# Row halves that exchange gate and up: a fused attention and feed-forward kernel

## The chip, the cores and the metric

The kernel runs on one core of a Trainium2 chip. Five engines work side by side from their own instruction queues: TensorE (PE in the profile; its weight loads are listed as PEld), VectorE (DVE), ScalarE (ACT), GpSimd (POOL) and SyncE (SP, which here only issues DMAs). They wait for each other through semaphores. The metric is the device time of one execution in microseconds. In the profile a line such as L375 is line 375 of the kernel before.

## The reference

```python
x = A_x                                   # [1, 2048, 448], bf16
xn = _layernorm(x)                        # (x - mean) / sqrt(var + 1e-5), no weights
# A: 16 query heads, 8 key/value heads, head size 256, the last W = 512 cached keys
q = (xn @ wq)                             # wq [448, 4096]
p = softmax(q k^T / 16)                   # over 512 keys, no mask
s = (p v) @ wo                            # wo [4096, 448]
# B: feed-forward, width 1792
g = silu((gelu_tanh(xn @ w_gate) * (xn @ w_up)) @ w_down)
return x + s * g
```

The inner size 448 is 3 x 128 + 64, or 7 x 64. That remainder is what the change is about: the array of TensorE has 128 rows.

## The kernel before, in words

The 2048 rows of x are cut into NQC = 4 chunks of QC = 512 rows, each of TPC = 4 tiles of 128. The program is recorded as a list of operations by `Rec.op`, one queue per engine, in the order in which the code issues them. `Rec` works out the semaphore waits from the tiles that an operation reads and writes; an operation on PE never waits for an earlier one on PE. Nothing reorders the work later, so the order in the code is the order on each engine.

*Start.* Four DMAs bring the tiles of chunk 0. DVE takes the statistics of all four (L293, L294), ACT the roots in two pairs (L335), and DVE the reciprocals (L338) and the normalized tiles (L299). PE, which has run 12 matmuls on zeros (`warm`, L308), transposes each tile with 14 transposes of 64 columns (L321), so that `xnT` holds each piece of 64 rows twice: on partitions 0 to 63 and again on 64 to 127. ACT copies two tiles out of PSUM (L327) and DVE two (L329). SP meanwhile issues the loads of the gate and up weights in four slices (`load_gu`, L238), gate to partitions 0 to 63 and up to 64 to 127, then w_down and the later chunks of x.

*Feed-forward, per chunk.* `gate_up(c, f)` handles one of NF = 14 blocks of 128 columns. For each of NK = 7 pieces of 64 rows it issues two matmuls (L375): gate in the lower row half of the array into one PSUM bank, up in the upper half into the next bank. The two run side by side. Three pairs of banks are used in turn. ACT applies gelu (L379) and DVE multiplies (L381). `down(c, t)` (L387) then makes the output of four tiles in banks 6 and 7. The later chunks are normalized on DVE among these blocks (`ln_later`, `ln_later2`), with GpSimd for the inverse root; DVE writes two copies of each normalized tile, and a transposing DMA issued by SP (L241) fills `xnT` in both halves. GpSimd issues the loads of wq, v and wo (`load_piece`) at fixed places, kept in step by a wait for PE.

*Attention.* Each of 64 (chunk, head) pairs has four slots, one for a tile of 128 queries: `scores` (L433, banks 4 and 5 in turn), the exponential with its sum on ACT (L437), reciprocal and scaling on DVE (L439, L440), a transposing DMA by SP, and, some 12 slots later, `values` (L453, mostly banks 0, 1 and 6) with a copy on DVE (L459), then `outproj` (L473, bank 7). `q_burst` projects queries in bursts of 4 or 8 half-pairs of heads, again with 7 pairs of 64-row matmuls (L418), two heads in the two row halves, into banks 0 to 3; ACT copies two banks at once (L422). The `down` tiles of the last chunk are put among slots 0 to 11 and 16 to 23 of this stage, in banks 6, 7, 7 and 2.

Of the kernel before, what the change touches and what calls it, by code (L numbers as in the profile page):

```python
# [11 lines left out]
P = 128  # L12
# [10 lines left out]
class Rec:  # L23
# [41 lines left out]
    def op(self, eng, fn, r=(), w=(), dma=False, after=(), lane=None):  # L65
# [17 lines left out]
        for d, raw in deps:  # L83
            if d.eng == eng and not d.dma and not dma and (eng == "tensor" or not raw and eng != "gpsimd"):
                continue
            d.inc = d.waited = True
            o.deps.append(d)
# [54 lines left out]
def bass_recurrent_scan__sliding_block_cached__geglu_ffn__prompt_kernel(nc, A_x, A_k, A_v, A_wq, A_wo, B_x, B_wg, B_wu, B_wd, out):  # L142
# [6 lines left out]
    QC, TPC, HP = 512, 4, 64  # L149
    NQC = S // QC  # L150
    NT = NQC * TPC
    NK = D // HP
    NF, NJ, NE = F // P, W // P, Dh // P
    assert S % QC == 0 and D % HP == 0 and NE == 2 and NJ == 4 and Hq == 2 * Hkv and Hq % 4 == 0 and NF % 2 == 0
# [4 lines left out]
    with es:  # L159
# [20 lines left out]
        xnT, _ = sb("xnT", [P, NQC, NK, QC], BF16)  # L180
# [3 lines left out]
        wq, _ = sb("wq", [P, NK, Hkv, Dh], BF16)  # L184
        wo, _ = sb("wo", [P, Hq * NE, D], BF16)
        gu_at = off[0]
        wgu, x_at = sb("wgu", [P, NK, F], BF16)
        x4, _ = sb("x4", [P, NT, D], BF16)
        NX = 4
        xn2, d_at = sb("xn2", [P, NX, NK, 2, HP], BF16)  # L190
# [16 lines left out]
        def fill_pr(at, end):  # L207
            while at + 2 * W <= end:
                t_, at = sb("pr%d" % len(pr), [P, W], BF16, at)
                pr.append(t_)  # L210
# [7 lines left out]
        for n in range(3, NQP):  # L218
            qT[n], at = sb("qT%d" % n, [P, 2, NE, QC], BF16, at)
        assert at >= hb_at, (at, hb_at)  # L220
        fill_pr(at, nc.sbuf_usable_end)
# [22 lines left out]
        dve(lambda e: e.memset(actT[:, NF - 1, :], 0.0), w=[("actT", NF - 1)])  # L244
# [8 lines left out]
        x0 = [dma("sync", x4[:, t, :], x_view[:, 0, t, :], w=[("x4", t)]) for t in range(TPC)]  # L253
        wg_v = B_wg.rearrange("(k p) f -> p k f", p=HP)
        wu_v = B_wu.rearrange("(k p) f -> p k f", p=HP)
        cuts = [0, 2, 6, 10, NF]
        fslice = {f: s for s in range(4) for f in range(cuts[s], cuts[s + 1])}

        def load_gu(s):
            a, b = cuts[s] * P, cuts[s + 1] * P  # L260
            dma("sync", wgu[0:HP, :, a:b], wg_v[:, :, a:b], w=[("wgu", 0, s)])
            dma("sync", wgu[HP:P, :, a:b], wu_v[:, :, a:b], w=[("wgu", 1, s)])
# [6 lines left out]
        for sl in range(4):  # L269
            load_gu(sl)  # L270
            if sl == 1:
                load_x(1)
        dma("sync", wd[:, :, :], B_wd.rearrange("(f p) d -> p f d", p=P), w=[("wd",)])
        for c in range(2, NQC):
# [5 lines left out]
        wq_v = A_wq.rearrange("(k p) (g two m) -> p k g two m", p=HP, two=2, m=Dh)  # L280
        pieces = [(wq[lo * HP:(lo + 1) * HP, k, :, :], wq_v[:, k, :, lo, :], ("wq", lo, k))
                  for k in range(NK) for lo in range(2)]
# [13 lines left out]
        def ln_norm(t, copies=2):  # L296
            s = t % NX
            for o in range(copies):
                dve(lambda e, o=o: e.tensor_scalar(  # L299
                    xn2[:, s, :, o, :], x4[:, t, :].rearrange("p (k d) -> p k d", k=NK), mv[:, t, 0:1],  # L300
                    rstd[:, t:t + 1], op0=ALU.subtract, op1=ALU.mult),
                    r=[("x4", t), ("mv", t), ("rstd", t)], w=[("xn2", s, o)])

        def warm(n):

            def run(e):
                for _ in range(n):
                    ins = e.matmul(bank(3), lhsT=actT[:, NF - 1, 0:P], rhs=actT[:, NF - 1, :], start=True, stop=True)  # L308
# [3 lines left out]
        def ln_tr(t):  # L312
            parts = ((act, 4),), ((dve, 5),), ((act, 6),), ((dve, 7),)
            parts = [(eng, b, 0, NK) for eng, b in parts[t]]
            for eng, b, a, z in parts:
                tp = bank(b).bitcast(BF16)

                def tr(e, tp=tp, a=a, z=z):
                    for k in range(a, z):
                        for lo in (0, HP):  # L320
                            ins = e.transpose(tp[lo:lo + HP, (k - a) * P:(k - a + 1) * P], xn2[:, t, k, 0, :], ident[:, :])  # L321
                    return ins
                pe(tr, r=[("xn2", t, 0), ("ident",)], w=[("ps", b)])
                dst = xnT[:, 0, a:z, t * P:(t + 1) * P]
                src = tp[:, 0:(z - a) * P].rearrange("p (k q) -> p k q", q=P)
                if eng is act:
                    act(lambda e, dst=dst, src=src: e.activation(dst, src, ACT.Copy), r=[("ps", b)], w=[("xnT", 0, t, a)])  # L327
                else:
                    dve(lambda e, dst=dst, src=src: e.tensor_copy(dst, src), r=[("ps", b)], w=[("xnT", 0, t, a)])  # L329

        for t in range(TPC):
            ln_stats(t)
            if t % 2:
                a, b = t - 1, t + 1
                act(lambda e, a=a, b=b: e.activation(std[:, a:b], mv[:, a:b, 1], ACT.Sqrt, bias=small[:, 0:1]),  # L335
                    r=[("mv", a), ("mv", t), ("eps",)], w=[("std", a)])
        for a in range(0, TPC, 2):
            dve(lambda e, a=a: e.reciprocal(rstd[:, a:a + 2], std[:, a:a + 2]),  # L338
                r=[("std", a)], w=[("rstd", a), ("rstd", a + 1)])
            ln_norm(a, 1)  # L340
# [262 lines left out]
```

## Time and profile before

| what | us |
|---|---|
| median of 3 runs (lowest to highest) | 559.74 (559.12 to 559.98) |
| the profiled execution: its own time | 558.75 |
| its span, first to last instruction | 557.0 |
| PE busy | 548.7 |
| DVE / ACT / POOL busy | 324.1 / 296.3 / 89.7 |
| gate/up of one chunk on the chain (196 matmuls) | 21.26 |
| down of one chunk (56 matmuls) | 10.70 |
| a burst of 8 on the chain (112 matmuls) | 12.19 |
| start of the first gate/up matmul | 9.28 |

Busy time counts an engine's instructions; matmuls are pipelined, so PE's share says that it never lacks work, not that it runs at its peak. The chain that ended last is followed back from the last instruction to what released each step. Lines of it are "start, length, what". Idle time of engines other than PE costs nothing as long as PE has its operands.

### The profile page before, as it was taken

Reading aid. Unit: us, or ns where it says so; the run is one execution under the profiler, and the core shown is the slowest. Engines: PE = TensorE matmul, PEld = TensorE weight load, DVE = VectorE, ACT = ScalarE, POOL = GpSimd, SP = SyncE. Lnnn points to the kernel's source line nnn. Section 1 sums busy time; section 2 is a strip of 40 time slices with the busy share of each in tenths; the row PEclk is TensorE's granted clock in tenths of the full one; section 3 lists DMA queues with packets and bytes.
Section 4 is the critical chain, followed back from the end, with each engine's and each line's share of the span. In section 5 each row is a group of like instructions: output and inputs, shape, how many; then the busy total and the mean of one; then the engine's idle time right before and its main releaser. Section 6 shows DMA issues by size and latency. Waiting matters only on the chain.

```text
span 557.0 us, 9857 instructions
## 1 busy us (share of the span) xinstructions
PE 548.7 (99%) x3498; PEld 258.8 (46%) x3532; DVE 324.1 (58%) x835; ACT 296.3 (53%) x673; POOL 89.7 (16%) x125
## 2 busy tenths in 40 slices
PE   8999999999999999999999999999999999999997
PEld 4544444444444444444444444444444444444445
DVE  5727446143462688078728744782688078638774
ACT  4423233247746665655575656556665655565631
POOL 0232323200000121001411110042121002411123
PEclk9999999999999999999999999999999999999999
DMA  8996846932453365245535542445354254634552
GB/s 196 276 177 102 138 102 143 264 110 70 95 87 67 67 96 98 46 94 104 112 81 95 104 86 44 100 92 137 75 96 100 34 95 97 120 88 98 93 95 52
DMA packets 169552, 58.83 MB, mean 106 GB/s; under 512 B 160160, under 2 KB 166432, under 8 KB 169504
## 3 DMA queue, kind: packets, MB, share of 16 engines
q1 hardware_dynamic: 166208, 45.50, 44.3%
q0 software_dynamic: 3152, 12.65, 8.7%
q8 instruction: 28, 0.46, 0.4%
q14 instruction: 20, 0.16, 0.1%
q10 hardware_dynamic: 144, 0.06, 0.0%
HBM read 17.92 MB, written 1.84 MB: 35 GB/s over the span
## 4 chain that ended last, share of the span: by engine, by line
PE 97%; DVE 2%; issue 1%; DMA 0%; ACT 0%
PE ps L453 20%; PE ps L433 20%; PE ps L418 18%; PE ps L473 17%; PE ps L375 15%; PE ps L387 8%; DVE tmp L482 0%; DVE xr L484 0%; DVE stats L293 0%; DMA x<-in_A_x_dram 0%; PE ps L321 0%; ACT xnT L327 0%; DVE mv L294 0%; DVE xn L299 0%; DVE rstd L338 0%
## 5 line engine op out<-in xcount | busy, mean ns | idle before, releaser
L437 ACT ACTIVATE pr<-ps 128x512 bf16<-128x512 f32 x256 | 152.7, 597 | 121.4 <-PE ps L433 117.9
L433 PE MATMUL ps<-kT,qT 128*128 128x512 bf16 x493 | 147.7, 379 | 2.0 <-issue 1.4
L453 PE MATMUL ps<-pT,V 128*128 128x512 bf16 x497 | 129.1, 379 | 0.8
L439 DVE RECIPROCAL rden<-den 128x1 f32<-128x1 f32 x256 | 41.5, 162 | 148.2 <-ACT pr L437 129.8
L473 PE MATMUL ps<-wo,oT 128*128 128x448 bf16 (+1 forms) x536 | 116.2, 344 | 0.0
L440 DVE TENSOR_SCALAR pr<-pr,rden 128x512 bf16<-128x512 bf16 x256 | 108.0, 422 | 9.0
L418 PE MATMUL ps<-xnT,wq 64*128 64x512 bf16 x896 | 98.3, 376 | 0.0
L422 ACT ACTIVATE qT<-ps 128x1024 bf16<-128x1024 f32 x64 | 65.5, 1023 | 40.6 <-PE ps L418 40.6
L375 PE MATMUL ps<-xnT,wgu 64*128 64x512 bf16 x784 | 85.3, 376 | 0.8 <-ACT xnT L327 0.8
L459 DVE CAST oT<-ps 128x512 bf16<-128x512 f32 x124 | 84.5, 682 | 0.7 <-PE ps L453 0.5
L453 PEld LDWEIGHTS ps<-pT,V 128*128 128x128 bf16 x512 | 50.0, 98 | 60.2 <-issue 0.3
L473 PEld LDWEIGHTS ps<-wo,oT 128*128 128x128 bf16 x536 | 52.4, 98 | 51.0
L433 PEld LDWEIGHTS ps<-kT,qT 128*128 128x128 bf16 x512 | 49.1, 98 | 55.8 <-issue 4.5
L381 DVE TENSOR_TENSOR actT<-ps,hb 128x512 bf16<-128x512 f32 x56 | 38.1, 685 | 57.2 <-ACT hb L379 55.3
L418 PEld LDWEIGHTS ps<-xnT,wq 64*128 64x128 bf16 x896 | 43.0, 94 | 54.6 <-DVE acc L494 2.5
L379 ACT ACTIVATE hb<-ps 128x512 bf16<-128x512 f32 x56 | 33.4, 597 | 51.4 <-PE ps L375 51.4
L375 PEld LDWEIGHTS ps<-xnT,wgu 64*128 64x128 bf16 x784 | 39.4, 94 | 46.0 <-issue 1.6
L437 ACT ACTIVATION_READ_ACCUMULATOR pr<-ps 128x1 f32 x256 | 49.8, 195 | 0.0
L387 PE MATMUL ps<-wd,actT 128*128 128x448 bf16 x224 | 46.2, 353 | 0.1
L498 POOL TENSOR_TENSOR tmp<-acc,gy 128x448 f32<-128x448 f32 x16 | 16.5, 1034 | 158.6 <-DVE acc L494 158.6
L513 POOL TENSOR_SCALAR tmp<-tmp 128x448 f32<-128x448 f32 x16 | 9.0, 563 | 187.8 <-ACT tmp L512 187.8
L387 PEld LDWEIGHTS ps<-wd,actT 128*128 128x128 bf16 x224 | 21.7, 98 | 22.2 <-issue 1.3
(43 smaller groups left out, 172.4 us busy)
## 6 DMA issues: line engine op xcount, KB each, us to landing
pT<-pr SPq DMA_TRANSPOSE x256, 2.4
wq<-in_A_wq_dram POOLq DMA_DIRECT2D x14, 256.0 KB, 5.2
wo<-in_A_wo_dram POOLq DMA_DIRECT2D x4, 896.0 KB, 6.6
V<-in_A_v_cache_dram POOLq DMA_DIRECT2D x4, 512.0 KB, 5.0
xr<-in_A_x_dram POOLq DMA_DIRECT2D x4, 448.0 KB, 3.9
wd<-in_B_w_down_dram SPq DMA_DIRECT2D x1, 1568.0 KB, 18.5
wgu<-in_B_w_gate_dram SPq DMA_DIRECT2D x3, 448.0 KB, 9.5
wgu<-in_B_w_up_dram SPq DMA_DIRECT2D x3, 448.0 KB, 11.1
```

The source lines that it names most:

```text
L375: ins = e.matmul(bank(b), lhsT=wgu[lo:lo + HP, k, f * P:(f + 1) * P], rhs=xnT[lo:lo + HP, c, k, :], start=k == 0, stop=k == NK - 1)
L381: dve(lambda e: e.tensor_tensor(actT[:, f, :], bank(s + 1), hb[:, n % NHB, :], ALU.mult), r=[("ps", s + 1), ("hb", n % NHB)], w=[("actT", f)])
L387: pe(lambda e, f=f: e.matmul(bank(b, D), lhsT=actT[:, f, t * P:(t + 1) * P], rhs=wd[:, f, :], start=f == 0, stop=f == NF - 1), r=[("actT", ...
L418: ins = e.matmul(bank(b), lhsT=wq[lo:lo + HP, k, h0 // 2 + hp, e_ * P:(e_ + 1) * P], rhs=xnT[lo:lo + HP, c, k, :], start=k == 0, stop=k == ...
L422: act(lambda e, e_=e_, s=s, buf=buf: e.activation(buf[:, :, e_, :], psum[:, s * 512:(s + 2) * 512].rearrange("p (a q) -> p a q", a=2), ACT ...
L433: ins = e.matmul(bank(b), lhsT=buf[:, a, k, t * P:(t + 1) * P], rhs=kT[:, g, k, :], start=k == 0, stop=k == NE - 1)
L437: act(lambda e: e.activation(pr[s][:, :], bank(b), ACT.Exp, scale=scale, accum_out=den[:, s:s + 1]), r=[("ps", b)], w=[("pr%d" % s,), ("de ...
L439: dve(lambda e: e.reciprocal(rden[:, s:s + 1], den[:, s:s + 1]), r=[("den", s)], w=[("rden", s)])
L440: dve(lambda e: e.tensor_scalar(pr[s][:, :], pr[s][:, :], rden[:, s:s + 1], None, op0=ALU.mult), r=[("pr%d" % s,), ("rden", s)], w=[("pr%d ...
L453: ins = e.matmul(bank(b), lhsT=V[:, j, g, e_ * P:(e_ + 1) * P], rhs=pT[:, i % NPT, j, :], start=j == 0, stop=j == NJ - 1)
L459: dve(lambda e: e.tensor_copy(dst, bank(b)), r=[("ps", b)], w=[key])
L473: ins = e.matmul(bank(b, D)[:, lo:hi], lhsT=oT[G % 2][:, idx, t * P:(t + 1) * P], rhs=wo[:, h0 * NE + idx, lo:hi], start=idx == 0, stop=id ...
```

## The change

The number of matmuls of each kind stays as it is, apart from the transposes and the warm-up. What changes:

- *Layout.* The first 384 of the 448 rows of gate, up and wq lie as three pieces of 128 rows on all partitions; the last 64 rows of gate (or of the first head) lie on partitions 0 to 63 and of up (or of the second head) on 64 to 127. `xnT` has four pieces instead of seven; only the last 64 rows are held twice.
- *Two phases.* A block runs phase 0: for each of the four pieces, gate on the lower row half and up on the upper half. Phase 1 covers the three full pieces with the halves exchanged, and adds into the same two banks. Phase 1 of a block is issued after phase 0 of the next, and waits for the end of its own phase 0 (`hard`). Four pairs of banks are used in the feed-forward, three in bursts of 8.
- *Start.* x comes in three DMAs. The first two tiles are normalized on GpSimd as soon as their own statistics are ready, the others on DVE. Transposes are 5 a tile, in banks 6 and 7 alone; ACT copies tiles 0 and 1, DVE 2 and 3. The warm-up is 50 matmuls of 128 columns. The weights come in three slices, with the last 64 rows in loads of their own.
- *Later chunks.* DVE writes one normalized copy; ACT copies its last 64 columns; `ln_later` and `ln_later2` move to other blocks.
- *Last chunk's down tiles.* Banks 6, 7, 3, 7; the last two tiles move from slots 16 to 23 to slots 13 to 20.
- *Memory.* Twelve buffers for probabilities; qT3 lies behind the feed-forward buffers.

```diff
-    def op(self, eng, fn, r=(), w=(), dma=False, after=(), lane=None):
+    def op(self, eng, fn, r=(), w=(), dma=False, after=(), lane=None, hard=()):
...
+        for d in hard:
+            d.inc = d.waited = True
+            o.deps.append(d)
...
-        xnT, _ = sb("xnT", [P, NQC, NK, QC], BF16)
+        xnT, _ = sb("xnT", [P, NQC, KF + 1, QC], BF16)
-        wq, _ = sb("wq", [P, NK, Hkv, Dh], BF16)
+        wq, _ = sb("wq", [P, KF, Hq, Dh], BF16)
+        wq6, _ = sb("wq6", [P, Hq // 2, Dh], BF16)
-        wgu, x_at = sb("wgu", [P, NK, F], BF16)
+        wg, _ = sb("wg", [P, KF, F], BF16)
+        wu, _ = sb("wu", [P, KF, F], BF16)
+        wgu6, x_at = sb("wgu6", [P, F], BF16)
-        xn2, d_at = sb("xn2", [P, NX, NK, 2, HP], BF16)
+        xn2, d_at = sb("xn2", [P, NX, D + HP], BF16)
...
-        dve(lambda e: e.memset(actT[:, NF - 1, :], 0.0), w=[("actT", NF - 1)])
+        dve(lambda e: e.memset(actT[:, NF - 1, 0:P], 0.0), w=[("actT", NF - 1)])
...
-        for sl in range(4):
-            load_gu(sl)
-            if sl == 1:
-                load_x(1)
+        load_x0(0, 1)
+        load_x0(1, 2)
+        load_x0(2, TPC)
+        load_gu6(0, 3)
+        load_gu(0)
+        load_gu6(3, NF)
+        load_gu(1)
+        load_x(1)
+        load_gu(2)
...
+        def ln_norm(t, eng=dve):
+            eng(lambda e: e.tensor_scalar(xn2[:, t % NX, 0:D], x4[:, t, :], mv[:, t, 0:1], rstd[:, t:t + 1],
+                                          op0=ALU.subtract, op1=ALU.mult),
+                r=[("x4", t), ("mv", t), ("rstd", t)], w=[("xn2", t % NX, 0)])
...
+        def ln_tr(t):
+            b = 6 + t % 2
+            tp = bank(b).bitcast(BF16)
+            def tr(e):
+                for k in range(KF):
+                    e.transpose(tp[:, k * P:(k + 1) * P], xn2[:, t, k * P:(k + 1) * P], ident[:, :])
+                for lo in (0, HP):
+                    ins = e.transpose(tp[lo:lo + HP, KF * P:(KF + 1) * P], xn2[:, t, KF * P:D], ident[:, :])
+                return ins
+            pe(tr, r=[("xn2", t, 0), ("ident",)], w=[("ps", b)])
...
+        def ln_first(t):
+            dve(lambda e: e.reciprocal(rstd[:, t:t + 1], std[:, t:t + 1]), r=[("std", t)], w=[("rstd", t)])
+            ln_norm(t, pool if t < 2 else dve)
+        warm(44)
+        ln_stats(0)
+        ln_std(0)
+        for t in range(1, TPC):
+            ln_stats(t)
+            ln_std(t)
+            if t < 3:
+                ln_first(t - 1)
+        for t in range(2, TPC):
+            ln_first(t)
+        warm(6)
+        ln_tr(0)
+        ln_copy(0)
...
+        def two_blocks(ph, c, s, w, w6, keys, q0=0, q1=QC):
+            def run(e):
+                for k in range(KF + 1 - ph):
+                    for lo in (0, HP):
+                        m = (lo > 0) ^ ph
+                        lhsT = w[m][lo:lo + HP, k, :] if k < KF else w6[lo:lo + HP, :]
+                        ins = e.matmul(bank(s + m)[:, q0:q1], lhsT=lhsT, rhs=xnT[lo:lo + HP, c, k, q0:q1],
+                                       start=ph == 0 and k == 0, stop=ph == 1 and k == KF - 1)
+                return ins
+            hard = [phase0[s]] if ph else []
+            phase0[s] = pe(run, r=xn(c)[q0 // P:q1 // P] + keys, w=[("ps", s), ("ps", s + 1)], hard=hard)
...
-            b = (6, 7, 7, 2)[t] if c == NQC - 1 else 6 + t % 2
+            b = (6, 7, 3, 7)[t] if c == NQC - 1 else 6 + t % 2
...
+            for n in range(heads + 1):
+                if n < heads:
+                    part(n, 0)
+                if n:
+                    part(n - 1, 1)
...
-            lead = 4 if c == 0 else 1
-            for f in range(NF):
-                gate_up(c, f)
...
+            lead = 6 if c == 0 else 2
+            for f in range(NF + 1):
+                if f < NF:
+                    gate_up(c, f, 0)
+                if f:
+                    gate_up(c, f - 1, 1)
...
-        for d, slots in ((0, range(0, 4)), (1, range(4, 12)), (2, range(16, 20)), (3, range(20, 24))):
+        for d, slots in ((0, range(0, 4)), (1, range(4, 12)), (2, range(13, 17)), (3, range(17, 21))):
```

## The prediction

> **What bounds the kernel now.** First the busy shares and the chain that ended last, to see which engine sets the time.
>
> ```profile
> span 557.0 us, 9857 instructions
> ...
> PE 548.7 (99%) x3498; PEld 258.8 (46%) x3532; DVE 324.1 (58%) x835; ACT 296.3 (53%) x673; POOL 89.7 (16%) x125
> ...
> PE 97%; DVE 2%; issue 1%; DMA 0%; ACT 0%
> ```
>
> PE is the whole chain. A change can help only by shortening PE's stream, by closing holes in it, or by starting it earlier. Next the chain in order of time over the first stage, which shows what PE waits for before its stream begins.
>
> ```profile
> 0.73 2.06 DMA x<-in_A_x_dram
> ...
> 5.92 0.52 DVE xn L299
> 6.44 0.04 issue
> 6.48 0.99 PE ps L321 x28
> 7.48 0.03 issue
> 7.51 0.60 PE ps L321 x14
> 8.11 0.02 issue
> 8.13 0.93 ACT xnT L327
> 9.06 0.22 issue
> 9.28 6.85 PE ps L375 x61
> ```
>
> The same chain over the whole span then shows stages without holes:
>
> ```profile
> 9.28 21.33 PE ps L375 x196
> 30.60 10.70 PE ps L387 x56
> 41.30 21.26 PE ps L375 x196
> ...
> 170.02 12.19 PE ps L418 x112
> ```
>
> The stream of useful matmuls starts at 9.28 us. From there 196 gate/up matmuls take 21.26 us: 98 pairs, one in each row half, at 0.217 us a pair. The projections of q run at 12.19 us for 112, 0.218 a pair. So both are bound by the columns streamed. The last view is the list of waits:
>
> ```profile
> PEld ps L433 <- ACT pr L437: 1.0, 4, 0.4
> ...
> PEld ps L375 <- ACT xnT L327: 0.9, 1, 0.9
> ```
>
> (total, times, longest). PE's weight loads for the scores wait for exponentials four times, all between 130 and 154 us and partly beside matmuls still streaming. Later only short holes at the changes between 64-row and 128-row operands remain, and those stay in number.
>
> **The pieces.** A block of 128 columns of gate and up had 7 pairs (NK = 7); now it has 4 in phase 0 and 3 in phase 1, again 7 with 512 columns each. So 392 pairs of L375 and 448 of L418 stay, and steady PE time moves by 0. That is the largest fact about this change.
>
> **The new wait.** Phase 1 of a block waits for its own phase 0 on PE's semaphore (120 waits: 56 blocks of the FFN, 64 of q). Behind it on PE are its 12 weight loads and matmuls and everything later; gelu (L379) or the copy of q (L422) waits for them. Between stands the next block's phase 0 and the previous block's phase 1, 7 pairs or 1.52 us; at the ends of a run 4 pairs (0.87) or 3 (0.65). A matmul of that kind ends 0.376 us after its start, 0.16 after its columns are in. So the wait is over 0.5 us before its turn in the tightest place. Before, the same engine waits for the product of the block three earlier (DVE L381), which ends 0.6 + 0.69 + about 0.15 us after the block's own pairs, about 1.6 us before the third next block begins, and the 21.26 us show no hole. I take 0; the upper end is a full exposed hand-over per wait, about 0.1 us (the chain has 0.06 of issue at 152.85, after a release that came just in time), 12 us in all; below 0 nothing, since a wait gains nothing.
>
> **The start.** I rebuild the chain. The first tile of x arrives at 2.79 as before. DVE's statistics come every 0.72 us (0.52 + 0.18 + 0.02 in the chain): mean and variance of tile 0 at 3.66, tile 1 at 4.38. Tile 0's root (ACT, 0.30) is under tile 1's statistics, its reciprocal ends near 4.45, and GpSimd normalizes it from 4.5. The cost there is not in the trace: nearest is GpSimd's tensor_scalar on 128x448 (L513, 563 ns), the other end its tensor_tensor (L498, 1034 ns). I take 0.56 (same kind): tile 0 ready at 5.1, tile 1 at 5.9; with 1.03 they are ready at 5.5 and 6.6. Queued behind it on GpSimd is nothing before the statistics of chunk 1. DVE meanwhile does the statistics of tiles 2 and 3 (to about 6.05, with two reciprocals) and norms 2 and 3 (0.5 each): 6.65 and 7.2, where the last norm before ended at 7.87.
>
> PE's warm-up goes from 12 matmuls of 512 columns to 50 of 128, all ahead of the transposes. The 512-column ones come every 0.43 us until the array's clock rises, so 0.107 each; the twelve took 4.95 us, less than 12 x 0.427 = 5.12, so the rise is near 5.7. From 1.05 (the memset is halved) 43 slow ones reach 5.65 and seven at half the time end near 6.05. All slow: 6.4. With a rise at 4.5: 5.5. So the first transpose goes at 6.05 and not at 5.1, and the early GpSimd norms are mostly wasted; 0.43 us ahead of today's 6.48 remain.
>
> A tile now has 5 transposes instead of 14; the row is 0.63 us from the first (6.48) to the copy that it releases (7.11). I take 0.5, ends 0.25 and 0.63. ACT's copy drops from 896 to 512 columns: 0.917 to about 0.60 (L379 reads 128x512 in 597 ns). DVE's drops from 620 ns to 0.42 (in proportion 0.35, unchanged 0.62). But only banks 6 and 7 are used: transposes of tile 2 wait for ACT's copy of tile 0, those of tile 3 for its copy of tile 1. Copy 0: 6.6 to 7.2; copy 1: to 7.8; transposes of tile 3: 7.85 to 8.35; copy 3 on DVE: to 8.8; first pair 0.1 later as in today's trace, 8.9. **Gain 0.4.** With the warm-up over at 5.5, norm 3 leads instead and the start is 8.4 (gain 0.9); with every matmul slow, the start is near 9.4 (loss 0.1).
>
> **The loads at the start.** Blocks 0 to 2 now need 98 KB of the last rows and 590 KB of the first 384 rows. SP issues 13 loads up to the last slice where it issued 12 with the same x1 among them (0.4 to 0.7 us each; the last went out at 8.11), so the landings count. Loads into 64 partitions ran slowly: the first gate slice (issued 2.59, 3.7 to landing) and up slice (3.37, 4.1) landed 1.2 us apart for 224 KB, 0.19 MB per us; the next three at 0.2. The load of w_down into 128 partitions, in packets of 896 B, took from 23.1 (the last up slice lands) to 27.6: 1.57 MB in 4.5 us, 0.35 per us. I take 0.35 for the 128-partition loads: blocks 0 to 2 by about 6.5, blocks 3 to 7 by 10.5, needed at 8.9 and 12.8. With 0.2 throughout they arrive at 7.7 and 14.4: a hole of 1.6 us. I take 0, for the nearer row has 128 partitions. The Trainium skill, in "DMA: Bandwidth & Descriptors", section "Rules for kernel authors", advises one 128-partition transfer over two to partition halves; the trace agrees (0.35 against 0.2), and by that rule this term is 0, by the other row +1.6.
>
> **Later tiles.** DVE makes one normalized copy instead of two (12 x 0.5 us less); ACT gets 12 copies of 64 columns, some 0.2 us each, that hold gelu back 0.5 us in alternate blocks, until norm is done. Banks now have four blocks' time (3.04 us between a block's last pair and their reuse), and 1.9 us are needed: hidden. The last transposed tile of chunk 1 is issued after block 13, about 32.2 instead of 31.2, and with the landing times of before, 2.9 to 10.1 us, is there between 35 and 42.3; it is needed at 40.9. As transposes now carry 512 rather than 896 columns and the loads are done sooner, I take 4 us: hidden, at worst 1.4 us exposed. The early gelu on ACT brings its table load (1.28) ahead of the first block: beside other work.
>
> **Attention.** Bursts of q now pass through banks 4 and 5, which the scores use. The tightest case is the first burst: its last two copies (1.02 us each) come together, so ACT is free 1.4 us after PE's last pair instead of 1.05; the third scores tile wants bank 4 2.3 us after that pair, and the first exponential with its sum (0.60 + 0.20) ends at 2.4. I charge 0.1. After bursts of 8 the slack is 0.3 us: 0. The down slots move from 16-23 to 13-20, under the stall after the burst at 144 to 150 us, which took about 0.2 (0.06 of it is "issue" at 152.85): gain 0.2. Slots 21 to 27, now bare, ask 0.86 us a slot of PE and 0.81 of ACT, as slots 24 to 27 did, without a hole. Weight loads of q, 14 DMAs on GpSimd, stay 14; SP has the same order of work. Buffers for probabilities grow; no wait for them is in the list, so 0.
>
> **Sum.** -0.4 - 0.2 + 0.1 = -0.5 us on the profiled 558.75 (span 557.0 and 1.75 around it): 558.25. The median of the runs, 559.74, is 0.99 higher; so **559.2 us**. A measurement of this kernel can tell about 0.2%, 1.1 us, from no change.
>
> **The rivals.**
> - *Faster, 558.3.* The warm-up ends early (start 8.4, gain 0.9) and the ordinary runs, 0.99 above the profiled one, lose part of that to weights: the second up slice lands at 12.0 and the third block wants it near 12.3, almost no reserve. Half of the 0.99 with 0.9: 1.4. For it: that reserve, and the faster loads. Against it: no hole in the trace at 12.3.
> - *Slower by the clock, 561.5.* After the warm-up PE has 20 transposes in 2.9 us instead of 56 in 2.8. If that counts as idle, or the clock has not yet risen, the first blocks run at half speed, for at most the 4.5 us that the rise took after PE's first matmul: half of that lost, 2.2, less the 0.5: 1.7. It decides if the first two pairs are 0.43 apart and not 0.217. Against it: today's hole of 0.77 us ahead of 9.28 does no harm. The Trainium skill, "TensorE: Matmul & The Clock Gate", section "HAM oscillation", lets the clock fall after about 3.4 us without matmuls; the bursts here keep gaps under 0.8 us, so by it this rival fails unless the rise comes late.
> - *Slower by the loads, 560.8.* Blocks 3 to 7 late by 1.6 us, if the rate stays under 2.0 MB in 8.5 us, 0.24 per us.
> - *Slower by the new wait, up to 571.* 120 x 0.1 us; against it the margin above.
>
> **How the numbers follow.** Forecast 0.48 (own range 558.7 to 560.2). Faster 0.27. Slower 0.25: clock 0.09, loads 0.07, the wait 0.05, a later tile or bank 0.04. The range 558.0 to 561.5 takes in the first rival and the two slower ones near it; it leaves out the new wait's 0.05 and some 0.13 in the tails.
>
> **What would show it.** First L375 pair near 8.9; warm-up's end near 6.05; tile 3's transposes released by ACT's second copy; 196 matmuls of gate/up still 21.3 us and 112 of q 12.2; PE waiting for no wg or wu load; a short wait of the third scores tile, none at 152. A chunk of gate/up above 21.6 us would make the steady part wrong.

## The result and the profile after

| | before | after |
|---|---|---|
| median of 6 runs each, us (lowest to highest) | 559.39 (558.81 to 559.98) | 562.69 (561.95 to 562.94) |
| ratio after / before, 95% interval | | 1.0055 (1.0041 to 1.0069) |
| profiled execution, us: its own time / its span | 558.75 / 557.0 | 561.95 / 560.1 |
| first gate/up matmul, us | 9.28 | 10.88 |

The changed kernel is 0.55% slower, some 3 us, where 0.5 us faster was forecast. Lines of the changed kernel have new numbers: L412 is the matmuls of gate, up and q (L375 and L418 before), L436 down (L387), L484 scores (L433), L504 values (L453), L320 the normalization (L299), L328 the warm-up, L338 and L340 the transposes, L349 and L351 their copies on DVE and ACT.

First the page of the changed kernel: its span, the busy time of the engines, the granted clock (PEclk: the share of full speed that TensorE was allowed, in tenths, in 40 equal slices of the span) and the chain by engine.

```profile
span 560.1 us, 9892 instructions
...
PE 552.3 (99%) x3534; PEld 259.8 (46%) x3534; DVE 317.5 (57%) x823; ACT 296.3 (53%) x688; POOL 91.9 (16%) x127
...
PEclk8999999999999999999999999999999999999999
...
PE 97%; DVE 1%; POOL 1%; issue 0%; DMA 0%; ACT 0%; DVEq 0%; POOLq 0%
```

PE still is the chain, and POOL is new in it. PE's busy time is 3.6 us higher, but that does not measure the loss: the trace before lacks some matmul records (493 of 512 for scores, 497 of 512 for values), the trace after has all of these. The first of the 40 slices of the clock has an 8 where the rest have 9 or more: some of the loss must lie within the first 14 us.

Next the chain of the changed kernel over the steady part (start, length, what).

```profile
33.83 10.70 PE ps L436 x56
44.52 21.26 PE ps L412 x196
65.78 10.70 PE ps L436 x56
...
147.62 6.15 PE ps L412 x56
...
173.09 12.19 PE ps L412 x112
```

Before, the same pieces began at 30.60, 41.30, 62.56 and so on, with the same lengths of 10.70 and 21.26. The first down begins 3.23 us later than before, the burst of queries at 147.62 also 3.23 (144.39 before), the burst at 173.09 only 3.07 (170.02 before), the end 3.1. So all of the loss stands at 33.83 us; the halves exchanged in two phases cost nothing in the 42 blocks of the later chunks; and the attention stage returned 0.16 by the second burst. Of the 3.23, 1.60 are the later first pair. The other 1.63 are lost between 10.88 and 33.83.

The chain of the changed kernel up to the first pair shows the first half of it:

```profile
4.67 0.98 POOL xn L320
...
6.53 1.97 POOL xn L320
...
8.55 0.34 PE ps L338 x3
...
9.11 0.60 ACT xnT L351
...
9.85 0.33 PE ps L338 x3
...
10.40 0.43 DVE xnT L349
...
10.88 9.13 PE ps L412 x67
```

Two GpSimd normalizations lead: the second ends at 8.5, then come tile 1's transposes (8.55), ACT's copy of tile 1, tile 3's transposes in the bank that it frees, DVE's copy. The instructions that write the tile xn in the changed kernel (durations in ns, shortest, median, longest; first and last start):

```profile
L320 POOL TENSOR_SCALAR xn<-x,mv,rstd x2: 1882/1922/1962, 4.7 to 6.5; 128x448 bf16<-128x448 bf16 x2
L320 DVE TENSOR_SCALAR xn<-x,mv,rstd x14: 386/387/521, 6.4 to 93.9; 128x448 bf16<-128x448 bf16 x14
```

One normalization takes GpSimd 1.92 us and DVE 0.39. The second half of the loss is in the table of stretches of the changed kernel:

```profile
core 0: us, PE busy (x) PEld busy (x) DVE busy (x) ACT busy (x) POOL busy (x), PEclk, DMA share, GB/s
...
10.00:11.00 1.00, 0.48 (x7) 0.24 (x7) 0.42 (x1) 1.00 (x1) 0.00 (x0) 0.89 1.06 366
11.00:12.00 1.00, 1.00 (x6) 0.30 (x6) 0.00 (x0) 0.21 (x2) 0.00 (x0) 0.50 1.05 392
...
13.00:14.00 1.00, 1.00 (x8) 0.44 (x6) 0.00 (x0) 0.00 (x0) 0.00 (x0) 0.50 1.05 375
14.00:15.00 1.00, 1.00 (x12) 0.38 (x8) 0.00 (x0) 0.00 (x0) 0.00 (x0) 0.90 1.09 378
```

The column behind POOL is the granted clock. It is 0.50 from about 10.78 (0.89 = 0.78 + 0.22 x 0.5) to 14.20, 3.4 us. PE's own timeline shows its two gaps ahead (in brackets, with what ended them) and the slow pairs behind:

```profile
6.60 0.34 PE L338 MATMUL ps<-ident,xn 128*128 128x128 bf16 x3 [1.26 <-POOL xn L320]
...
8.55 0.34 PE L338 MATMUL ps<-ident,xn 128*128 128x128 bf16 x3 [1.43 <-POOL xn L320]
...
10.88 0.61 PE L412 MATMUL ps<-xnT,wg 64*128 64x512 bf16 x1 [0.52 <-DVE xnT L349]
...
11.28 0.63 PE L412 MATMUL ps<-xnT,wg 64*128 64x512 bf16 x1
...
14.24 0.38 PE L412 MATMUL ps<-xnT,wu 64*128 64x512 bf16 x1
```

The first eight pairs come up to 0.43 us apart instead of 0.217. They take 3.36 us, from 10.88 to 14.24, where eight pairs at full clock take 1.74: 1.62 us more, which is the 1.63.

The theory at this point: (a) GpSimd's normalization is three times as long as was priced and delays the start; (b) PE, idle while it waits, loses its clock, and the first blocks pay for that. The rivals: that the exchanged halves or the waits cost something at the beginning; that only one of (a) and (b) matters; and, for (a), that the duration is a collision with DVE and not GpSimd's own.

### The profile page after: what moved, and what is told of

It reads as the page before. It is cut to its first block, busy times and chain, and to the rows that moved or that the text cites. A ratio compares the mean times of both kernels' runs of the same rounds, so it can differ in the third digit from the quotient of the medians.

```text
span 560.1 us, 9892 instructions
## 1 busy us (share of the span) xinstructions
PE 552.3 (99%) x3534; PEld 259.8 (46%) x3534; DVE 317.5 (57%) x823; ACT 296.3 (53%) x688; POOL 91.9 (16%) x127
## 4 chain that ended last, share of the span: by engine, by line
PE 97%; DVE 1%; POOL 1%; issue 0%; DMA 0%; ACT 0%; DVEq 0%; POOLq 0%
PE ps L412 33%; PE ps L484 20%; PE ps L504 20%; PE ps L524 16%; PE ps L436 8%; POOL xn L320 1%; DVE tmp L533 0%; DVE xr L535 0%; DMA x<-in_A_x_dram 0%; DVE stats L316 0%; PE ps L338 0%; ACT xnT L351 0%; DVE xnT L349 0%; PE ps L340 0%; DVE mv L317 0%
## 5 line engine op out<-in xcount | busy, mean ns | idle before, releaser
L488 ACT ACTIVATE pr<-ps 128x512 bf16<-128x512 f32 x256 | 152.6, 598 | 119.9 <-PE ps L484 118.6
L484 PE MATMUL ps<-kT,qT 128*128 128x512 bf16 x512 | 151.9, 380 | 0.0
L504 PE MATMUL ps<-pT,V 128*128 128x512 bf16 x512 | 131.2, 380 | 0.0
L412 PE MATMUL ps<-xnT,wq 64*128 64x512 bf16 x896 | 98.3, 377 | 0.0
L412 PE MATMUL ps<-xnT,wg 64*128 64x512 bf16 x336 | 83.4, 381 | 0.5 <-DVE xnT L349 0.5
L412 PE MATMUL ps<-xnT,wu 64*128 64x512 bf16 x336 | 83.7, 381 | 0.0
L504 PEld LDWEIGHTS ps<-pT,V 128*128 128x128 bf16 x512 | 50.0, 98 | 60.1 <-issue 0.3
L484 PEld LDWEIGHTS ps<-kT,qT 128*128 128x128 bf16 x512 | 49.2, 98 | 55.4 <-issue 4.0
L412 PEld LDWEIGHTS ps<-xnT,wq 64*128 64x128 bf16 x896 | 43.1, 94 | 54.4 <-DVE acc L545 2.5
L488 ACT ACTIVATION_READ_ACCUMULATOR pr<-ps 128x1 f32 x256 | 50.2, 196 | 0.0
L436 PE MATMUL ps<-wd,actT 128*128 128x448 bf16 x224 | 46.2, 353 | 0.0
L412 PEld LDWEIGHTS ps<-xnT,wg 64*128 64x128 bf16 x336 | 31.6, 95 | 21.4 <-issue 2.2
L412 PEld LDWEIGHTS ps<-xnT,wu 64*128 64x128 bf16 x336 | 31.6, 95 | 20.2 <-issue 0.5
```

Source lines behind the costliest of these rows:

```text
L412: ins = e.matmul(bank(s + m)[:, q0:q1], lhsT=lhsT, rhs=xnT[lo:lo + HP, c, k, q0:q1], start=ph == 0 and k == 0, stop=ph == 1 and k == KF - 1)
L436: pe(lambda e, f=f: e.matmul(bank(b, D), lhsT=actT[:, f, t * P:(t + 1) * P], rhs=wd[:, f, :], start=f == 0, stop=f == NF - 1), r=[("actT", ...
L484: ins = e.matmul(bank(b), lhsT=buf[:, a, k, t * P:(t + 1) * P], rhs=kT[:, g, k, :], start=k == 0, stop=k == NE - 1)
L488: act(lambda e: e.activation(pr[s][:, :], bank(b), ACT.Exp, scale=scale, accum_out=den[:, s:s + 1]), r=[("ps", b)], w=[("pr%d" % s,), ("de ...
L504: ins = e.matmul(bank(b), lhsT=V[:, j, g, e_ * P:(e_ + 1) * P], rhs=pT[:, i % NPT, j, :], start=j == 0, stop=j == NJ - 1)
```

## The experiments

**Tiles 0 and 1 on DVE (e1), and the gaps filled (e2, e3).** In e1 `ln_first` normalizes on DVE throughout. e2 keeps GpSimd and puts matmuls on zeros between the transposes, as the warm-up has them, so that PE has no long gaps. e3 does both.

```diff
 # e1 and e3
-            ln_norm(t, pool if t < 2 else dve)
+            ln_norm(t)
 # e2 (in e3: none more ahead; 8, 14, 2 and 9 behind the tiles)
-        warm(6)
+        warm(22)
         ln_tr(0)
+        warm(26)
         ln_copy(0)
         ...
         ln_tr(2)
+        warm(6)
         ln_copy(2)
         ln_tr(3)
+        warm(8)
```

> The changed kernel with the first two tiles normalized by DVE, nothing else undone. Theory: GpSimd's two norms, 1.9 us each in the trace of after, set the start at 10.88 us, and PE's idle time behind them lets its clock fall for one 3.4 us stretch, which costs another 1.7 us. Then DVE's chain (statistics, four norms of 0.4 to 0.5 us, copy) gives a first gate/up pair near 9.3 us, the clock stays up, and the median is 559.3, as before. Rival 1: the clock falls because there are only 20 transposes after a short warm-up, whoever normalizes; then the first pair is at 9.3 but eight pairs still come 0.43 us apart, and the median is 561.0. Rival 2: the two-phase blocks cost time in the steady part; then nearly 562.

> The changed kernel with GpSimd's norms kept, and 56 more warm-up matmuls of 128 columns put into PE's idle times (16 ahead of the first tile's transposes, 26, 6 and 8 behind those of tiles 0, 2 and 3). Theory: idle time lets the clock fall; now it stays up, the first pair is still near 10.9 us, all pairs come 0.217 us apart, and 1.7 us of the 3.3 are gone: median 561.0. Rival: the fall has nothing to do with idle time; then eight pairs at 0.43 us again and 562.7. If the fillers hold back the transposes, the first pair is later than 11.

> Norms on DVE and fillers (8, 14, 2, 9 behind the four tiles' transposes). Theory: the two causes add and nothing else is left: first pair near 9.3, no slow pair, median 559.2 (the move of the down slots is worth 0.1 to 0.2). If rival 2 of the run with DVE norms alone is right, over 560.

| kernel | norm of tiles 0, 1 | gaps | us (median of 11) | ratio to before | first pair, profiled run |
|---|---|---|---|---|---|
| after (6 runs) | GpSimd | open | 562.69 | 1.0055 (1.0041 to 1.0069) | 10.88 |
| e2 | GpSimd | filled | 560.55 | 1.0021 (1.0012 to 1.0031) | 10.95 |
| e1 | DVE | open | 558.97 | 1.0006 (0.9995 to 1.0017) | 9.32 |
| e3 | DVE | filled | 559.19 | 1.0002 (0.9993 to 1.0011) | 9.47 |

The chain of e2 shows that its start is as late as that of the changed kernel and is set by the same GpSimd instruction:

```profile
4.75 1.89 POOL xn L320
...
10.95 7.05 PE ps L415 x64
```

Its clock was 1.00 from 11 to 12 us, where the changed kernel had 0.50. So the clock alone is worth 0.0034 of 559, 1.9 us (the two intervals leave about 1 us either way), and the late start alone, e2 against e3, 560.55 - 559.19 = 1.4 us (1.48 by the first pairs). Together they are the loss, and with both gone (e3) nothing is left: the first chunk, too, takes 21.26 us there, and the two phases, the 120 waits and the layout cost nothing that can be measured (the interval of e3 reaches to 0.6 us). In e1 the clock was expected to stay up; it is a matter of chance instead, although no gap of PE ahead of the first pair is longer than 0.76 us in the profiled execution: four of its 11 executions have a mean clock of 0.997 and take 560.35 to 560.48, seven have 0.999 or 1.0 and take 558.75 to 559.03. The profiled one is of the four; its second microsecond after the first pair:

```profile
10.00:11.00 1.00, 1.00 (x6) 0.31 (x4) 0.00 (x0) 0.00 (x0) 0.00 (x0) 0.50 1.02 357
```

**What makes GpSimd slow (e5, e10, e11).** Three kernels add operations on GpSimd to the changed kernel in the down phase of the second chunk, where DVE has no normalization to do; nothing uses their results. e5 asks whether the time comes from DVE beside it or from the two operands per partition; e10 whether it comes from the types; e11 changes the operation itself. One execution each.

```diff
 # e5; x4 is bf16, mv and rstd are one f32 per partition
+  tensor_scalar(probe0, x4, mv, rstd, op0=subtract, op1=mult)      # L594
+  tensor_scalar(probe1, x4, 0.25, 2.0, op0=subtract, op1=mult)     # L596
+  tensor_scalar(probe2, x4, mv, None, op0=subtract)                # L598
+  tensor_scalar(probe3, x4, mv, 2.0, op0=subtract, op1=mult)       # L600
 # e10; pf is f32, pb bf16
+  tensor_scalar(pf0, x4, 0.25, 2.0, op0=subtract, op1=mult)        # L596
+  tensor_scalar(pf1, pf0, mv, rstd, op0=subtract, op1=mult)        # L598
+  tensor_scalar(pb0, pf0, 0.25, 2.0, op0=subtract, op1=mult)       # L600
+  tensor_scalar(pf1, pf0, 0.25, 2.0, op0=subtract, op1=mult)       # L602
 # e11
+  tensor_scalar(pb0, x4, 1.0, 0.5, op0=add, op1=mult)              # L596
+  tensor_scalar(pb1, x4, rstd, mv, op0=mult, op1=add)              # L598
+  tensor_scalar(pb2, x4, mv, rstd, op0=add, op1=mult)              # L600
+  tensor_scalar(pf0, x4, 1.0, 0.5, op0=add, op1=mult)              # L602
+  tensor_scalar(pf0, pf0, 0.25, 2.0, op0=subtract, op1=mult)       # L604
```

> The changed kernel with four more GpSimd operations on 128x448 bf16, written to unused memory, behind the first down tile of chunk 1, where DVE is busy for 0.7 of 10.7 us: the norm itself (subtract and multiply by two per-partition pointers), the same with two constants, one pointer alone, and a pointer with a constant. Theory 1: two pointers make the operation dear by themselves; then the norm takes 1.9 us here too, the constants 0.56 as L513 of before does, one pointer in between. Theory 2: DVE's statistics beside it made it slow at the start; then the norm takes about 0.6 us here. The time of the kernel stays as it was, since PE is not held up.

> The changed kernel with four GpSimd tensor_scalar operations on 128x448 in the quiet place behind the first down tile of chunk 1: bf16 to f32 with constants, f32 to f32 with two pointers, f32 to bf16 with constants, f32 to f32 with constants. Theory: the data type makes the norm dear, since bf16 with constants took 1.72 us and f32 in place (tmp) 0.56; then the all-f32 ones take 0.56 to 0.7 and those with bf16 on a side 1.1 to 1.7. Rival: what is cheap about the row on tmp is something else, and all four take 1.4 us or more.

> The changed kernel with five more GpSimd operations on 128x448 in the same quiet place: bf16 to bf16 with two constants, add then multiply (the operators of the row on tmp); bf16 to bf16 with two pointers, multiply then add; the same, add then multiply; bf16 to f32 with constants, add then multiply; and f32 in place with constants, subtract then multiply. Types and pointers changed little so far (1.72 to 1.88 us), so what is left for the 0.56 of the row on tmp is its operators or that it works in place. Theory: a leading subtract is the dear part; then the four operations without it take 0.56 to 0.75 and the last 1.7. Rival: working in place is the cheap part; then the last takes 0.56 and the others 1.7.

The groups of instructions on GpSimd of e5 (busy us, mean ns of one, then the idle time before it):

```profile
L594 POOL TENSOR_SCALAR probe<-x,mv,rstd 128x448 bf16<-128x448 bf16 x1 | 1.9, 1877 | 2.7 <-PE ps L437 2.7
L600 POOL TENSOR_SCALAR probe<-x,mv 128x448 bf16<-128x448 bf16 x1 | 1.8, 1797 | 0.0
L596 POOL TENSOR_SCALAR probe<-x 128x448 bf16<-128x448 bf16 x1 | 1.7, 1722 | 0.1
L598 POOL TENSOR_SCALAR probe<-x,mv 128x448 bf16<-128x448 bf16 x1 | 1.4, 1418 | 0.0
```

DVE does nothing from 69 to 78 us, while these run, and the norm takes 1.88 again, so a collision is not the cause; constants save only 0.15. Two operations, or a value per partition, would explain the 1.42 to 1.88 among these four, but not a factor of three against 0.563. Of e10, with f32 in and out (L598), and f32 in and bf16 out (L600):

```profile
L598 POOL TENSOR_SCALAR pf<-pf,mv,rstd 128x448 f32<-128x448 f32 x1 | 1.9, 1875 | 0.1
...
L600 POOL TENSOR_SCALAR pb<-pf 128x448 bf16<-128x448 f32 x1 | 1.7, 1724 | 0.0
```

The types change nothing, so that theory fell too. Of e11:

```profile
L604 POOL TENSOR_SCALAR pf<-pf 128x448 f32<-128x448 f32 x1 | 1.7, 1736 | 0.1
...
L600 POOL TENSOR_SCALAR pb<-x,mv,rstd 128x448 bf16<-128x448 bf16 x1 | 0.7, 710 | 0.0
L596 POOL TENSOR_SCALAR pb<-x 128x448 bf16<-128x448 bf16 x1 | 0.6, 564 | 2.7 <-PE ps L439 2.7
```

It is the leading subtract: with add and mult the same shape, types and operands take 0.71 in place of 1.88, and with constants 0.56 in place of 1.72. The row of before that gave the price is this one:

```profile
L513 POOL TENSOR_SCALAR tmp<-tmp 128x448 f32<-128x448 f32 x16 | 9.0, 563 | 187.8 <-ACT tmp L512 187.8
```

In the code it is `tensor_scalar(..., 1.0, 0.5, op0=ALU.add, op1=ALU.mult)`: an add, with constants, which is the 0.56 of L596 here. The row does not name the arithmetic; the code line does.

**The normalization with an add (e12), and with the gaps filled as well (e13).** GpSimd first negates the two means (128x1), and then adds. e13 adds fillers of 7, 5, 0 and 8.

```diff
+            if eng is pool:
+                pool(lambda e: e.tensor_scalar(xn2[:, t, 0:D], x4[:, t, :], nmean[:, t:t + 1], rstd[:, t:t + 1],
+                                               op0=ALU.add, op1=ALU.mult), ...)
+                return
...
+            if t == 1:
+                for u in range(2):
+                    pool(lambda e, u=u: e.tensor_scalar(nmean[:, u:u + 1], mv[:, u, 0:1], -1.0, 0.0, op0=ALU.mult, op1=ALU.add), ...)
```

> The changed kernel with only the form of GpSimd's two norms altered: add the negated mean, then multiply, in place of subtract and multiply (two more GpSimd operations of 128x1 make the negated means). By the operations measured alone it costs 0.71 instead of 1.88 us. Theory: the price of that one operation was the step of the prediction that failed; with it the two norms end near 5.4 and 6.4, the first gate/up pair comes at 8.8 to 8.9, as predicted, and executions whose clock stays up take 558.3 to 558.6. PE still idles between its warm-up and the first block, so some executions lose up to 1.7 us to the clock, as with the norms on DVE (4 of 11). Rival: the start stays above 10, then the norms were not what set it.

> The same with fillers behind the transposes of tiles 0, 1 and 3 (7, 5 and 8 matmuls of 128 columns). Theory: first pair at 8.8 to 8.9 and no execution loses its clock; weights of blocks 3 to 7, landing near 12.3, are just in time (wanted near 12.7). Median 558.4, ratio 0.999 or a little less. If the loads are late, a hole of up to 0.5 us near 12.7 and no gain left.

e12 took 558.63 us against 559.11, ratio 0.9988 (0.9979 to 0.9997), with a clock of 0.999 or 1.0 in all 11 executions, where some had been expected to lose it (PE's gaps are not filled, but the longest is 0.53 us in the profiled execution). It is faster than the changed kernel, and by about half a microsecond than before; the interval just excludes no change, and reaches to 0.21%. e13 took 558.91, ratio 1.0000 (0.9991 to 1.0009). The engine timeline of e12 for GpSimd, and its chain into the first pair:

```profile
3.80 0.19 POOL L376 TENSOR_SCALAR nmean<-mv 128x1 f32<-128x1 f32 x1 [2.28 <-DVE mv L318]
...
4.99 1.50 POOL L322 TENSOR_SCALAR xn<-x,nmean,rstd 128x448 bf16<-128x448 bf16 x2
```

```profile
6.63 0.49 ACT xnT L357
...
8.39 0.43 DVE xnT L355
...
8.87 9.23 PE ps L422 x83
```

Two norms take 1.50 instead of 3.83, and the first pair goes at 8.87. GpSimd has left the chain; ahead of ACT's copy of tile 0 now stand DVE's statistics and ACT's last root (6.34 to 6.63). With e13 the first pair goes at 8.74 but PE stops for 0.17 at 12.77, just where block 3, the first of the second slice, begins, so nothing is won by it.

**The other ways to an earlier start (e4, e8, e9).** e4 gives tiles 0 and 1 to ACT (scale and bias per partition), loads x in four DMAs, transposes into banks 4 to 7 and fills the gaps. e8 adds to e4 that ACT issues the loads of the last 64 rows, ahead of x; e9 instead leaves them on SP, in one piece behind the first slice.

```diff
 # e4 (fillers: 7 behind tile 0, 2 behind tile 1, 8 behind tile 3)
+            dve(lambda e: e.tensor_scalar(nmr[:, t:t + 1], mv[:, t, 0:1], rstd[:, t:t + 1], -1.0, op0=ALU.mult, op1=ALU.mult), ...)
+            act(lambda e: e.activation(xn2[:, t, 0:D], x4[:, t, :], ACT.Identity, scale=rstd[:, t:t + 1], bias=nmr[:, t:t + 1]), ...)
...
-            b = 6 + t % 2
+            b = 4 + t
...
-        load_x0(2, TPC)
+        load_x0(2, 3)
+        load_x0(3, TPC)
 # e8, on top of e4
-                dma("sync", wgu6[...
+                dma("scalar", wgu6[...
-        load_gu6(0, 3)
+        load_gu6(0, NF)
         load_gu(0)
-        load_gu6(3, NF)
 # e9, on top of e4
-        load_gu6(0, 3)
         load_gu(0)
-        load_gu6(3, NF)
+        load_gu6(0, NF)
```

> A version meant to beat both: the first two tiles normalized on ACT (scale and bias by pointers, with one more DVE op of 128x1 each), the four x tiles in four loads, transposes in banks 4 to 7 instead of 6 and 7, fillers 7, 2 and 8 behind tiles 0, 1 and 3. Theory: the start is a chain of norms and copies; DVE's last norm ends near 7.5, first pair at 8.5, clock up, median 558.5. If ACT's norm costs more than 0.6 us or needs a table load (1.28), the first pair is at 9.3 or later and the median 559.3 or more.

> The version with norms on ACT, with the last 64 rows of gate and up loaded whole by two DMAs issued from ACT, so that SP reaches the slices of 128 partitions some 2 us earlier. That version lost 0.5 us at 12.86, where PE waited for the weights of blocks 3 to 7 (issued 6.17 and 6.80, landed by 13.3). Theory: those now land by 12 and the hole is gone; first pair at 8.8 or a little sooner, median 0.4 to 0.5 us under the 558.99 of that version, 558.5. If the loads are bound by bytes and not by their issue, the hole stays.

> The version with norms on ACT again, all loads on SP behind the four x tiles, but the last 64 rows of gate and up whole in two DMAs behind the first slices of 128 rows, so that the slices of blocks 3 to 7 are issued some 1.2 us earlier and nothing runs ahead of x. Theory: x lands as before (tile 1 by 3.4), the first pair is at 8.8, the hole of 0.5 us at 12.86 is gone or under 0.1, and the median is 0.8 to 0.9 us under the kernel before, ratio 0.9985. If the bytes and not the issue set the landing, the hole stays and the ratio is 0.999.

| kernel | us | ratio to before | first pair, profiled run |
|---|---|---|---|
| e4 (11 runs) | 558.99 | 0.9989 (0.9972 to 1.0006) | 8.79 |
| e8 (7) | 561.17 | 1.0028 (1.0005 to 1.0052) | 11.74 |
| e9 (12) | 559.41 | 0.9998 (0.9979 to 1.0016) | 10.11 |

All three missed what was hoped of them, and in each a load that had been in time came late. In the chain of e4 PE starts early and then has a hole at block 3:

```profile
8.79 4.06 PE ps L423 x36
12.86 0.50 issue
13.36 4.69 PE ps L423 x41
```

The up weights of blocks 3 to 7 were issued at 6.80 and took 6.5 us, to 13.3, which is where the hole ends. In e9 the tiles were ready by about 9.0, and PE waited 1.0 us for the last 64 rows of up, issued at 4.21 and landing 5.77 later. In e8 those loads went out beside x, and the second tile of x landed at 5.37, where it had landed at 3.86 in e12; PE stood still for 1.77 us for it, and in four of the seven executions the clock fell as well (0.997 and 0.993), in spite of the fillers. Both first pairs ahead of 8.8 (e4, and e13 above) met a hole at block 3; that of e12, at 8.87, did not. It looks as if the bytes set this limit, but no run varies the bytes alone, so that stays open.

**GpSimd in the kernel before (e7).** If the norm alone is to blame, the kernel before must become slower with it, by some 2 to 4 us.

```diff
-            ln_norm(a, 1)
-            ln_norm(a + 1, 1)
+            ln_norm(a, 1, dve if a else pool)
+            ln_norm(a + 1, 1, dve if a else pool)
```

> The kernel before with its first two tiles normalized on GpSimd, nothing else. If GpSimd's norm costs 1.9 us whatever the layout, its two run from about 5.95 to 9.75 us, tile 1 is transposed and copied last on DVE, and the first gate/up pair comes near 11.6: 2.3 us more, and up to 1.7 on top in executions in which the clock falls in the wait: median 561.4 to 563.1. If the price belongs to the new layout (0.56 here), the first pair is near 9.3 and the median as before.

It took 564.88 us, ratio 1.0097 (1.0082 to 1.0112): more than expected. Its chain, and its stretches:

```profile
6.32 3.76 POOL xn L299 x2
...
10.12 1.73 PE ps L321 x28
...
13.34 8.85 PE ps L375 x53
```

```profile
9.00:10.00 1.00, 0.00 (x0) 0.00 (x0) 0.00 (x0) 0.80 (x1) 1.00 (x1) 0.50 1.16 226
10.00:12.00 2.00, 1.88 (x36) 1.88 (x38) 0.62 (x1) 0.13 (x1) 0.07 (x1) 0.50 1.10 246
...
18.00:20.00 2.00, 2.00 (x16) 0.95 (x14) 0.00 (x0) 0.56 (x1) 0.00 (x0) 0.71 1.16 208
```

The two norms take 3.76. PE idles so long that the clock falls at 8.9 already, ahead of most transposes, which then take 1.73 instead of 0.99, and it is back at 19.2: 10.2 us at half. The cause stands; its price depends on how long the clock stays down.

**The down tiles back in slots 16 to 23 (e6).** One execution.

```diff
-        for d, slots in (..., (2, range(13, 17)), (3, range(17, 21))):
+        for d, slots in (..., (2, range(16, 20)), (3, range(20, 24))):
```

> The changed kernel with the last two down tiles back in slots 16 to 23 (banks 6, 7, 3, 7 kept). If the move of the slots closed the hole of the scores near 152 us, it is back: PE waits some 0.1 to 0.3 us more between 150 and 154 us than in the changed kernel, and nothing else differs. The start is the same (near 10.9, slow pairs).

In the chain of e6 the burst that begins at 147.62 in the changed kernel begins at 149.11. Between it and the next burst PE waits for an exponential on ACT (L488), ahead of the scores (L484):

```profile
149.11 5.52 PE ps L412 x50
...
156.48 0.70 ACT pr L488 x2
...
157.22 0.60 PE ps L484 x2
...
175.00 5.07 PE ps L412 x45
```

From burst to burst that is 25.89, against 25.47 in the changed kernel (173.09 - 147.62) and 25.63 before (170.02 - 144.39). So, by one execution each, the earlier slots are worth 0.42, more than the 0.1 to 0.3 that was expected, and the rest of the change at this place costs 0.26. What the 0.26 is made of was not looked into. The total, 564.22, says nothing about the slots: in this execution the first pair went at 11.43, 0.55 later than in the changed kernel's profiled one, and the mean clock was 0.994 where that had 0.997.

## Why the prediction was wrong

The step that failed is the cost of GpSimd's normalization: "I take 0.56 (same kind): tile 0 ready at 5.1, tile 1 at 5.9; with 1.03 they are ready at 5.5 and 6.6". Measured: 1.88 to 1.97 each, ready at 6.55 and 8.5. Both rows that were to bound the cost from two sides were of the wrong operation, and the true price lay outside both ends; that is why the sum and the range missed together. "Same kind" was judged by the name of the instruction and the shape; the arithmetic operation in it decided. With the cost the path fell too: the forecast had the end of the warm-up release the first transpose, "and the early GpSimd norms are mostly wasted", but PE waited 1.26 us for tile 0 and 1.43 for tile 1. With an operation whose cost is near the one assumed (e12, 0.71), the sum holds nearly to the number: first pair 8.87 against 8.9, 0.48 us faster than before against 0.5. That agreement is in part luck: the chain into it runs through DVE's statistics and ACT's queue, not through the end of the warm-up.

The rival "slower by the clock" then came true on top, and its sign was given: the first pairs are 0.40 to 0.43 apart. It was held at 0.09 because "the bursts here keep gaps under 0.8 us". In the changed kernel that fell with the failed step: PE's gaps were 1.26 (after the warm-up) and 1.43 us (before tile 1's transposes). But it was no safe ground in itself: in e1 the gaps were under 0.8, as was forecast, and the clock fell in four of 11 executions. The size, 2.2, was near the 1.6 of the profiled run and the 1.9 of e2. The rule that the prediction weighed there, the Trainium skill's "TensorE: Matmul & The Clock Gate", section "HAM oscillation", wants no idle gap over about 3.4 us. The traces do not agree as far as one gap goes: the longest here was 1.43 us, in e1 0.76, and the clock fell. What does agree is 3.4 us as the length of the stretch.

The other steps, in the order of the prediction:

- *The pieces, 0.* Right: 196 matmuls in 21.26 and 112 in 12.19, as before.
- *The new wait, 0 with an upper end of 12 us.* Right: the later chunks have 21.26 and 10.70 as before, and e3 has nothing left over.
- *The warm-up's end, 6.05 with bounds 5.5 and 6.4.* Too late for the profiled run: 5.34. The same 50 matmuls took 4.37 us there, 4.89 in e12 and 5.28 in e1, so the clock rises at another moment from one execution to the next, and no single number was right.
- *Transposes 0.5, copies 0.60 and 0.42, and the order in which tile 3 waits for ACT's second copy.* Right: 0.54, 0.60, 0.43, and the chain shows that order.
- *The loads, 0.* Right in the sum, wrong in the reserve. PE waited for no weights in the changed kernel, but blocks 3 to 7 of up landed at 12.3 (issued 6.32, 6.0 to landing) and not by 10.5. Between 11 and 15 us the DMAs moved 375 to 392 GB/s, near the 0.35 MB per us that was taken; the slices were not alone on them. e4 shows the hole that a start at 8.8 can meet, 0.5 us.
- *Attention, -0.2 and +0.1.* The net is right, -0.16 against -0.1; both terms were too small, 0.42 and 0.26.
- *Later tiles hidden.* Right: no wait of PE between the chunks.

## What to carry to other kernels

A price from a row counts only if the row does the same arithmetic on the same engine; where no such row exists, the range has to reach past the neighbours, and a cheap way to write the same formula (add the negated mean) is worth a try before the engine is blamed. Ahead of a dense stream of matmuls, a late operand can be paid for twice, once by the wait and once by the clock, and a bound on the longest gap did not guard against that here; a look at the clock of every execution does tell. When a start is moved earlier, look at what the weights' landing leaves, since here PE stopped for them as soon as it started at 8.7 to 8.8.

## What the hardware showed unexpectedly

- A tensor_scalar on GpSimd, 128x448, takes 1.72 to 1.96 us with a leading subtract followed by mult and 1.42 with a subtract alone, and 0.56 (constants) to 0.71 (values per partition) with add and mult. Neither the types nor working in place changes it. On DVE the norm with the subtract takes 0.39 to 0.40 alone; beside GpSimd's norms the two took 0.59 and 0.60 in e2 and 0.41 and 0.52 in the changed kernel, and why they differ is open.
- The clock goes down for whole stretches of 3.41 us: one in the profiled run of the changed kernel (10.78 to 14.20) and in e1 (9.28 to 12.70), two in e5 (9.38 to 16.20), three in e7 (8.94 to 19.18). One stretch shows as a mean clock of 0.997 and two as 0.994, and five of the six runs of the changed kernel have 0.994: they take 562.55 to 562.94, while the profiled one, with 0.997, takes 561.95. The profiled run is thus the cheapest of the six. The second stretch does not cost as much as the first: in e5, which starts like the changed kernel, part of the 6.8 us falls on PE's waiting and 5.2 lie behind the first pair at 11.04, and its execution is 1.07 us longer than the profiled one. The kernel before is not immune: three of some 90 executions have 0.997 or 0.993, and take 563.46 to 564.96.
- The warm-up's matmuls come 0.107 us apart until about 4.0 in the profiled run of the changed kernel and until about 5.9 in e1 and e5, and 0.056 apart behind (the column of the granted clock reads 1.00 throughout). The falls come 6.8, 3.4 and 3.4 us after that. All this fits a check at fixed intervals of 3.41 us, which start at another moment in each execution; then it is chance, as in e1, whether a quiet stretch fills an interval. What the check asks is open. PE's busy time alone does not sort the stretches: the changed kernel kept its clock after one with 1.90 us busy (3.96 to 7.37) and lost it after one with 1.47 (7.37 to 10.78), but e1 lost it after one with 2.17 (5.87 to 9.29). None of this was put to an experiment of its own. That filling the gaps prevents the fall was (e2, e3: no fall in 22 executions), though not where x came late (e8).
